# Attention and two MoE layers on one core: loads of q and k in three parts, and the copy of the tails behind VectorE's decoding step

## The chip, the cores and the metric

The kernel runs on one core of a Trainium2 chip. The metric is the device time of one execution in microseconds; an execution that was profiled has, beside its time, a span from its first to its last instruction. TensorE multiplies matrices, VectorE, ScalarE and GpSimd work on elements, and SyncE issues nearly all of the DMA transfers. Each of them runs its own instructions in order; between engines the order is kept by semaphores.

## The reference

All inputs are 32-bit floats; the weights of the two MoE layers are 64-bit floats that the kernel decodes itself. Cut to what is computed:

```python
scores = scale * np.matmul(q, k.transpose(0, 1, 3, 2))      # 4 batches, 8 heads, 576 rows, 64 wide
rel = (pos[:, None] - pos[None, :]).astype(np.float32)
x = (np.log1p(np.abs(rel)) / psi_i)[..., None]
bias = np.maximum(x @ w1 + b1, 0.0) @ w2                    # one bias for each head
scores = scores + bias.transpose(2, 0, 1)[None]
attn = np.exp(scores - scores.max(-1, keepdims=True))
attn = attn / (attn.sum(-1, keepdims=True) + 1e-09)
x = np.matmul(attn, v)                                      # then rows of 2304 tokens, 512 wide
h = np.maximum(np.maximum(x @ w1, x @ w2), x @ w3)          # first layer, 768 wide
x = h @ w_out
h = x @ w_in                                                # second layer, 2048 wide
out = np.where(h > 0, h, np.exp(np.minimum(h, 0)) - 1) @ w_out
```

## The kernel before

A prologue makes the bias and stores it in DRAM (to about 62 us of the profiled span). Then the attention runs (to about 335 us), then the first MoE layer (to about 626 us) and the second. The change touches the attention alone.

The attention has 16 pairs of heads, numbered n, and each has five steps, c = 0 to 4, so there are 80 steps s = 5n + c. Four of them have 128 query rows of both heads; c = 4 has the last 64 rows of both, in one half. The order of the work is written out by hand. Each piece of work is put on a list with a due time in steps (`at`, line 548); the list is sorted by that time (line 591), and each engine's queue is filled in that order. The due times set an order, not a clock: an engine starts its next instruction as soon as the semaphores allow it.

The pieces of step s that matter, with the table `OFF` (line 35), are these. `unit_qk` (line 216) has TensorE multiply q and k into the PSUM tile `PB[0]` for h = 0 and `PB[1]` for h = 1. `scores` (line 225) is VectorE's reduction of that product with the bias tile; it writes `e_t`. `expo` is ScalarE's exponential. `recip` and `diag` make reciprocals of sums (VectorE) and diagonal tiles (GpSimd, line 249). Two steps later `trans` transposes the exponentials into `TQ` on TensorE, and `tails` (line 262) transposes the last 64 columns into two spare 64-column corners of `PB[0]`. `evac_tails` (line 299) is VectorE's copy of these corners to SBUF; it is the 128x128 COPY of line 77 in the trace (64x128 in c = 1, which handles the tail of a c = 4 step). `evac` copies `TQ`: ScalarE does it, but VectorE does one half where the source step has c = 0 or 2, which falls into the running steps c = 2 and 4. `pv` multiplies by v, and `x_copy`, `x_sum`, `x_hi`, `x_lo` finish an output block, the last two on GpSimd (lines 73 and 81).

`pump` (line 471), due at 0.32 in every step from 7 on except c = 1, takes the decoder of the MoE weights one piece further. A piece is one VectorE instruction on 128x512 integers (lines 420, 423, 425, 427, 430, in turn), at times with a fetch of raw weights (line 371) or a store of finished ones (line 466) on SyncE's queue, and with ScalarE or GpSimd work of splitting.

So in one step VectorE's order is: scores of h = 0, reciprocals of the step before, in c = 0 and 2 the sum of an output block (line 345), scores of h = 1, copy of the tails (due at 2.311 of its own step, which is 0.311 in the running one), decoding piece (0.32), in c = 2 and 4 the copy of one half of `TQ`. TensorE's is: products of q and k for both h, transposes, tails, products with v, and then the products of the next step, whose first half writes `PB[0]` again.

`load_kq` (line 94) brings the 864 KB of q and k of a pair into one of two buffers, `load_v` (line 98) the 320 KB of v into one of two. They are due at 5n + 0.2 for the pair n + 1, and 5n + 6.2, which is one step into that pair. The tile of q and k has k in its first 576 columns and the two heads' q in the second and third 576.

Of the kernel before, what the change touches and what calls it, by code (L numbers as in the profile page):

```python
# [11 lines left out]
F32 = mybir.dt.float32  # L12
# [19 lines left out]

OFF = {"qk0": 0.0, "qk1": 0.01, "t0": 0.02, "ns": 1.025, "dg": 1.026, "t1": 0.03, "tr": 2.10, "tl": 2.20, "evt": 2.311,
       "pump": 0.32, "ev0": 2.385, "ev1": 2.387, "ex0": 0.38, "ex1": 0.40}
PV_AT = {1: [(4.5, 0), (4.5, 1), (5.5, 2), (5.5, 3), (5.5, 4)],
         4: [(3.5, 0), (3.5, 1), (4.5, 2), (4.5, 3), (5.5, 4)]}
# [15 lines left out]
def fused_kernel(ctx, tc, tkq, vv, lt, pk, wm1, wo1, win2, wo2, out):  # L54
    nc = tc.nc
# [34 lines left out]
    kq = att.enter_context(tc.tile_pool(name="kq", bufs=2))  # L90

    KQ, TV = {}, {}

    def load_kq(n):
        KQ[n] = kq.tile([128, 1728], F32, tag="kq", name="kq_t")
        nc.sync.dma_start(KQ[n], tkq[n])

    def load_v(n):
        TV[n] = ld.tile([128, 640], F32, tag="tv", name="tv_t")
# [21 lines left out]
    with ExitStack() as pro:  # L121
# [18 lines left out]
        with tc.manual_schedule():  # L140
            nc.sync.dma_start(pk_t, pk)
            nc.sync.dma_start(lt_t[:, 512:1148], lt[:, 512:1148])
            nc.sync.dma_start(lt_t[:, 0:512], lt[:, 0:512])
            load_kq(0)
            load_v(0)
            nc.vector.tensor_scalar(nbt, psi_t, b1_t, -1.0, op0=ALU.mult, op1=ALU.mult)
# [401 lines left out]
    def at(key, fn, *args):  # L548
        plan.append((key, len(plan), fn, args))

    for s, (n, c) in enumerate(steps):
        o = {nm: s + off for nm, off in OFF.items()}
        at(o["qk0"], unit_qk, s, 0)
# [22 lines left out]
        if n % 4 == 3 and n < 15:  # L576
            at(s + 0.45, load_b, n // 4 + 1, c)
    for n in range(4 * NP - 1):
        at(5 * n + 0.2, load_kq, n + 1)
        at(5 * n + 6.2, load_v, n + 1)  # L580
    at(3.05, fetch)
    at(3.05, fetch)
    for i in range(6):
# [317 lines left out]
```

## Time and profile before

| | us |
|---|---|
| median of 3 runs | 1014.34 |
| lowest and highest run | 1010.53, 1014.87 |
| profiled execution, its time | 1010.22 |
| its span | 1008.4 |
| TensorE busy in the span | 977.4 |
| VectorE busy | 692.1 |
| ScalarE busy | 526.1 |
| GpSimd busy | 341.7 |

Busy times are sums over the whole span, over stages with different limits. Below, TensorE is PE (its weight loads PEld), VectorE DVE, ScalarE ACT, GpSimd POOL, and SyncE's queue SPq. In a row of the timeline the numbers ahead are start and duration in microseconds, "xN" is how many instructions were merged into it, and a bracket at its end holds the engine's idle time before it and what ended that. "issue" in the chain of waits is time in which an engine waited for nothing that the profile shows.

### The profile page before, as it was taken

The page shows a single profiled execution, that of the slowest core. Times are in us where ns is not written, and L with a number is a line of the kernel's source. Part 1 is how long each engine was busy: PE and PEld are TensorE (multiplying, and loading weights), DVE is VectorE, ACT ScalarE, POOL GpSimd, SP SyncE. Part 2 cuts the span into 40 slices and gives each one's busy share as a digit, 9 for nine tenths or more (in the row PEclk, how much of TensorE's full clock was granted, in tenths as well). Part 3 has the DMA queues.
Part 4 walks back from the last instruction along what each step waited for, and adds up shares of the span by engine and source line. Part 5 has one row for each costly group of instructions (what it writes and reads, how often), then busy time and mean ns, then how long its engine had stood idle before and what let it go on. Part 6 is the DMA issues. An engine that isn't in the chain of part 4 may idle for free.

```text
span 1008.4 us, 28525 instructions
## 1 busy us (share of the span) xinstructions
PE 977.4 (97%) x11748; PEld 869.2 (86%) x11748; DVE 692.1 (69%) x1428; ACT 526.1 (52%) x1087; POOL 341.7 (34%) x419
## 2 busy tenths in 40 slices
PE   7979899999999999999999999999999999999998
PEld 4447777778887899999999999998998989988996
DVE  7967778788886699887887862835574355743342
ACT  8967777777775233333333331644445344453443
POOL 0013344344343354534553550323232132321222
PEclk9989999999999999999999999999999999999999
DMA  7842724645532356879886981355657556575553
GB/s 259 291 172 85 247 94 157 205 163 187 176 127 79 134 187 215 308 234 341 321 282 236 328 298 47 116 189 175 199 192 252 191 171 204 188 258 185 176 197 105
DMA packets 65905, 201.00 MB, mean 199 GB/s; under 512 B 7024, under 2 KB 14832, under 8 KB 65776
## 3 DMA queue, kind: packets, MB, share of 16 engines
q1 hardware_dynamic: 65776, 199.18, 57.6%
q8 instruction: 93, 1.52, 0.6%
q14 instruction: 36, 0.29, 0.1%
HBM read 150.78 MB, written 48.37 MB: 197 GB/s over the span
## 4 chain that ended last, share of the span: by engine, by line
PE 91%; DVE 6%; issue 1%; DMA 1%; ACT 0%; SPq 0%; POOL 0%; DVEq 0%; POOLq 0%; ACTq 0%
PE xo L696 18%; PE pb L740 13%; PE pb L526 12%; PE tq L740 6%; PE tq L252 6%; PE xo L319 6%; PE xo L526 5%; PE tq L526 5%; PE pb L222 5%; PE pb L620 4%; PE pb L183 3%; PE pbb L183 2%; DVE e_t L230 2%; PE xo L620 2%; PE tq L620 2%
## 5 line engine op out<-in xcount | busy, mean ns | idle before, releaser
L81 POOL TENSOR_TENSOR gl<-t_t,gh 128x384 fp32r<-128x384 f32 x96 | 108.7, 1142 | 286.3 <-ACT gh L75 286.3
L235 ACT ACTIVATE e_t<-e_t,st_t 128x576 f32<-128x576 f32 x144 | 111.4, 773 | 58.6 <-DVE st_t L240 56.1
L230 DVE CUSTOM_DVE_ANT_0 e_t<-pb,b_t 128x576 f32<-128x576 f32 x144 | 107.7, 749 | 32.7 <-PE pb L222 32.5
L249 POOL TENSOR_SCALAR dg_t<-ident,st_t 128x64 f32<-128x64 f32 x144 | 48.1, 348 | 212.7 <-DVE st_t L241 93.2
L740 PE MATMUL pb<-w_t,gh 128*128 128x512 f32 x384 | 119.3, 392 | 0.0
L526 PE MATMUL pb<-xh,w_t 128*128 128x384 f32 x448 | 116.8, 336 | 0.0
L252 PEld LDWEIGHTS tq<-dg_t,e_t 64*64 64x64 f32 x4608 | 96.6, 136 | 22.7 <-issue 7.7
L252 PE MATMUL tq<-dg_t,e_t 64*64 64x64 f32 x4608 | 97.8, 222 | 10.9 <-issue 5.3
L696 PE MATMUL xo<-tt,w_t 128*128 128x384 f32 x528 | 107.4, 338 | 0.0
L718 ACT ACTIVATE t_t<-c_t 128x384 f32<-128x384 f32 x96 | 50.0, 521 | 103.4 <-DVE c_t L709 95.6
L222 PE MATMUL pb<-kq_t 64*64 64x288 f32 x1152 | 98.6, 413 | 3.8 <-issue 1.3
L696 PEld LDWEIGHTS xo<-tt,w_t 128*128 128x128 f32 x528 | 95.0, 188 | 7.7 <-issue 0.3
L696 PE MATMUL xo<-xh,w_t 128*128 128x384 f32 x328 | 94.6, 335 | 0.0
L319 PE MATMUL xo<-p,tv_t 64*64 64x320 f32 (+1 forms) x1024 | 85.4, 408 | 1.6 <-issue 1.2
L526 PEld LDWEIGHTS pb<-xh,w_t 128*128 128x128 f32 x448 | 81.1, 188 | 0.5 <-issue 0.4
L740 PEld LDWEIGHTS pb<-w_t,gh 128*128 128x128 f32 x384 | 70.5, 188 | 6.6
L740 PE MATMUL pb<-w_t,gl 128*128 128x512 f32 x192 | 75.5, 393 | 0.0
L526 PE MATMUL pb<-xl,w_t 128*128 128x384 f32 x224 | 75.3, 336 | 0.0
L75 ACT ACTIVATE p<-tq 128x512 f32<-128x512 f32 (+1 forms) x128 | 62.8, 528 | 16.4 <-PE tq L252 15.2
L222 PEld LDWEIGHTS pb<-kq_t 64*64 64x64 f32 x1152 | 50.9, 133 | 22.9 <-DVE p L77 4.4
L75 ACT ACTIVATE gh<-t_t 128x384 fp32r<-128x384 f32 x96 | 48.6, 519 | 33.4 <-DVE t_t L726 33.4
L696 PEld LDWEIGHTS xo<-xh,w_t 128*128 128x128 f32 x328 | 60.2, 188 | 3.0
(131 smaller groups left out, 2198.1 us busy)
## 6 DMA issues: line engine op xcount, KB each, us to landing
w_t<-scw_w SPq DMA_DIRECT2D x90, 512.0 KB, 4.4
w_t<-scw_wi SPq DMA_DIRECT2D x74, 512.0 KB, 4.2
kq_t<-tkq SPq DMA_DIRECT2D x16, 864.0 KB, 5.4
scw_wi<-sp SPq DMA_DIRECT2D x26, 512.0 KB, 4.7
scw_w<-sp SPq DMA_DIRECT2D x22, 512.0 KB, 5.5
raw<-wo SPq DMA_DIRECT2D x22, 512.0 KB, 3.7
scr<-o_t SPq DMA_DIRECT2D x36, 288.0 KB, 3.9
raw<-wm SPq DMA_DIRECT2D x18, 512.0 KB, 4.1
```

Source lines behind the costliest of these rows:

```text
L75: nc.scalar.activation(dst, src, AF.Copy)
L81: e.tensor_tensor(out=dst, in0=src, in1=hi.bitcast(F32), op=ALU.subtract)
L183: mm(p[32 * a4:32 * a4 + 32, 224 + 288 * hf:512 + 288 * hf], w28, FT[A, a4][:, 288 * hf:288 * hf + 288], start=True, stop=True)
L222: mm(PB[h][H64[g], 224 + 288 * r:512 + 288 * r], t[H64[r], 576 + 576 * a + q0:640 + 576 * a + q0], t[H64[r], 288 * a:288 * a + 288], start ...
L230: nc.vector.tensor_tensor_reduce(out=E[s][:, 576 * h:576 * h + 576], in0=PB[h][:, 224:800], in1=BT[n // 4, c, h], op0=ALU.add, op1=ALU.min ...
L235: nc.scalar.activation(e, e, AF.Exp, bias=st[:, h:h + 1], scale=-1.0, accum_out=st[:, 2 + h:3 + h])
L252: mm(dst, E[s][H64[g], k0:k0 + 64], DG[s][H64[g], h % nheads(s)], start=True, stop=True)
L319: mm(XO[g][H64[h], 0:w], v[H64[g], 128 * k + 64 * h:128 * k + 64 * h + 64], ps[0][H64[g], 4 * h + k, :], start=(k == 0), stop=(k == 3 and ...
L526: mm(ps[blk][:, 0:NB], wt[:, ks], xt[:, kk, t0:t0 + NB], start=(j == 0), stop=(j == 11))
L620: mm(ps[blk][:, 0:NB], WO[0][:, kk, wt, ms], xt[:, bs], start=(j == 0), stop=(j == 3 * NM1 - 1))
L696: mm(ps, w[wt][:, ks], b[xt][:, kk], start=(start and j == 0), stop=(stop and j == 5), skip_group_check=True)
L740: mm(acc[t], g[:, ts], w[k], start=(f == 0 and i == 0 and j == 0), stop=(f == NU - 1 and i == 1 and j == 2))
```

## The change

Two things are changed. The copy of the tails gets the due time 2.33 in place of 2.311, which is 0.33 in the running step and so behind the decoding piece at 0.32. The load of q and k is issued in three parts of 576 columns (288 KB each), due at 5n + 1.2, 2.2 and 3.2 in place of one of 864 KB at 5n + 0.2, and the load of v is due a step later, at 5n + 7.2.

```diff
-OFF = {... "tr": 2.10, "tl": 2.20, "evt": 2.311,
+OFF = {... "tr": 2.10, "tl": 2.20, "evt": 2.33,
        "pump": 0.32, "ev0": 2.385, "ev1": 2.387, "ex0": 0.38, "ex1": 0.40}
...
-    def load_kq(n):
-        KQ[n] = kq.tile([128, 1728], F32, tag="kq", name="kq_t")
-        nc.sync.dma_start(KQ[n], tkq[n])
+    def load_kq(n, i=None):
+        if not i:
+            KQ[n] = kq.tile([128, 1728], F32, tag="kq", name="kq_t")
+        cs = slice(576 * i, 576 * i + 576) if i is not None else slice(0, 1728)
+        nc.sync.dma_start(KQ[n][:, cs], tkq[n][:, cs])
...
     for n in range(4 * NP - 1):
-        at(5 * n + 0.2, load_kq, n + 1)
-        at(5 * n + 6.2, load_v, n + 1)
+        for i in range(3):
+            at(5 * n + 1.2 + i, load_kq, n + 1, i)
+        at(5 * n + 7.2, load_v, n + 1)
```

## Rows read from the trace of the kernel before

**Rows 1.** The page's first part: busy time, share of the span, instructions of each engine.

```profile
PE 977.4 (97%) x11748; PEld 869.2 (86%) x11748; DVE 692.1 (69%) x1428; ACT 526.1 (52%) x1087; POOL 341.7 (34%) x419
```

**Rows 2.** Busy time by stretch; columns: PE, PEld, DVE, ACT, POOL, clock, DMA, GB/s.

```profile
128.00:144.00 16.00, 15.94 (x485) 12.99 (x477) 14.07 (x43) 11.92 (x29) 6.12 (x14) 1.00 0.39 144
```

**Rows 3.** Waits of PEld, 60 to 340 us: total, times, longest.

```profile
PEld pb L222 <- DVE p L77: 4.4, 14, 0.6
```

**Rows 4.** Timeline of steps 21 and 22 (c = 1 and 2), DVE and PE.

```profile
130.05 0.28 DVE L77 COPY p<-pb 64x128 f32<-64x128 f32 x1
...
131.38 0.76 DVE L230 CUSTOM_DVE_ANT_0 e_t<-pb,b_t 128x576 f32<-128x576 f32 x1 [1.05 <-PE pb L222]
...
133.34 0.28 DVE L77 COPY p<-pb 128x128 f32<-128x128 f32 x1
...
133.54 0.68 DVE L425 SCALAR_TENSOR_TENSOR t_w<-raw,t_w 128x512 int32<-128x512 int32 x1
...
133.69 1.38 PE L222 MATMUL pb<-kq_t 64*64 64x288 f32 x16
134.14 0.68 DVE L77 COPY p<-tq 128x512 f32<-128x512 f32 x1
...
134.74 0.75 DVE L230 CUSTOM_DVE_ANT_0 e_t<-pb,b_t 128x576 f32<-128x576 f32 x1
```

**Rows 5.** Timeline of steps 23 and 24 (c = 3 and 4), DVE and PE.

```profile
136.41 0.29 DVE L77 COPY p<-pb 128x128 f32<-128x128 f32 x1
...
136.95 0.76 PE L222 MATMUL pb<-kq_t 64*64 64x288 f32 x8
...
137.77 0.76 DVE L230 CUSTOM_DVE_ANT_0 e_t<-pb,b_t 128x576 f32<-128x576 f32 x1 [0.47 <-PE pb L222]
...
139.00 0.29 DVE L77 COPY p<-pb 128x128 f32<-128x128 f32 x1 [0.19 <-PE pb L252]
...
140.41 0.75 DVE L230 CUSTOM_DVE_ANT_0 e_t<-pb,b_t 128x576 f32<-128x576 f32 x1
```

**Rows 6.** Timeline of step 30 (c = 0), DVE and POOL.

```profile
160.15 0.29 DVE L77 COPY p<-pb 128x128 f32<-128x128 f32 x1
160.19 0.87 POOL L81 TENSOR_TENSOR xl<-xf,xh 128x320 fp32r<-128x320 f32 x1
160.35 1.25 DVE L430 TENSOR_TENSOR t_w<-t_w,x_t 128x512 int32<-128x512 int32 x1
...
161.53 0.74 DVE L230 CUSTOM_DVE_ANT_0 e_t<-pb,b_t 128x576 f32<-128x576 f32 x1
```

**Rows 7.** Timeline of step 27 (c = 2), with GpSimd's split of a weight.

```profile
150.04 0.40 POOL L73 TENSOR_SCALAR xh<-xf 128x256 fp32r<-128x256 f32 x1
...
150.21 0.29 DVE L77 COPY p<-pb 128x128 f32<-128x128 f32 x1
150.41 1.28 POOL L81 TENSOR_TENSOR w_t<-t_w,w_t 128x512 fp32r<-128x512 f32 x1
150.41 1.56 DVE L423 TENSOR_SCALAR t_w<-raw 128x512 int32<-128x512 int32 x1
...
152.49 0.74 DVE L230 CUSTOM_DVE_ANT_0 e_t<-pb,b_t 128x576 f32<-128x576 f32 x1
```

**Rows 8.** Groups of DVE, 66 to 320 us: count, busy us, mean ns, idle.

```profile
L420 DVE TENSOR_SCALAR x_t<-raw 128x512 int32<-128x512 int32 x13 | 6.5, 505 | 0.0
```

**Rows 9.** Timeline of SyncE's queue: loads of one pair.

```profile
204.49 0.33 SPq L96 DMA_DIRECT2D kq_t<-tkq  x1
206.24 0.33 SPq L100 DMA_DIRECT2D tv_t<-vv  x1
```

**Rows 10.** Chain of waits, attention: start, us, what; three of twelve such pieces.

```profile
76.33 0.67 issue
...
210.64 1.15 issue
...
298.83 0.35 issue
```

More of the change, by code (lines that the diff above doesn't have):

```diff
@@ L30 @@
 BIG = 3.0e38
-OFF = {"qk0": 0.0, "qk1": 0.01, "t0": 0.02, "ns": 1.025, "dg": 1.026, "t1": 0.03, "tr": 2.10, "tl": 2.20, "evt": 2.311,
+OFF = {"qk0": 0.0, "qk1": 0.01, "t0": 0.02, "ns": 1.025, "dg": 1.026, "t1": 0.03, "tr": 2.10, "tl": 2.20, "evt": 2.33,
        "pump": 0.32, "ev0": 2.385, "ev1": 2.387, "ex0": 0.38, "ex1": 0.40}
```

## The prediction

> **What bounds the kernel now.** I read the page first, then busy time by stretch, then the chain of waits and the timeline of single attention steps. On the page PE is busy 97% of the span [rows 1], and inside the attention a quiet stretch shows 15.94 of 16 us [rows 2]. So whatever makes PE wait in the attention lengthens the whole, and the MoE stages behind are only shifted. The chain has PE nearly everywhere, with two kinds of exceptions: DVE pieces, and pieces named "issue", where PE stands still with no semaphore to wait for. Of the latter above 0.3 us there are twelve, from 76 to 299 us, and they sum to 9.6 us [rows 10].
>
> The timeline shows what ties two steps together. PE's products of q and k for the next step write the PSUM tile from which DVE copies the tails, and they wait for that copy: the waits name it [rows 3], and in step 22 the copy runs from 133.34 to 133.62 and the first product starts at 133.69 [rows 4]. I compared all 77 pairs of steps from 2 to 78: never does the product start sooner than 0.05 us after the copy's end, and in 55 it starts within 0.12 us of it. From the copy's start to the product it is 0.35 us, and from the product to the next scores on DVE 0.82 us (136.95 to 137.77) [rows 5]. Hence a loop: copy, products, scores, copy, with **1.17 us** from the copy's start to the next scores. The decoding piece now lies beside that stretch, behind the copy; DVE would otherwise wait there, as it does 1.05 us in the step without a piece [rows 4].
>
> **The swap on DVE.** It removes and adds no instruction. It puts the piece ahead of the copy, so the copy, and PE behind it, wait for the piece. Wherever the tails are there when the scores end, that is a serial cost; 40 of 58 steps with a piece have the copy without any idle time ahead. What I compare is the time from now's start of the copy to the next scores, now against (piece + 1.17).
>
> A two-input piece (lines 425, 427, 430) shows 0.68 us, but its successor starts after 0.60 (133.54 to 134.14) [rows 4]; I use 0.60.
> - c = 2: now 133.34 to 134.74, 1.40 us [rows 4]. Then 0.60 + 1.17 = 1.77: +0.37, eight times, +3.0.
> - c = 3: now 136.41 to 137.77, 1.36 us [rows 5]. Then 1.77: +0.41, eight times, +3.3.
> - c = 4: the copy now waits 0.19 us for the tails, so the piece can start at 138.81; the next scores come at 138.81 + 1.77 = 140.58 in place of 140.41 [rows 5]: +0.17, six times, +1.0.
> - c = 0: now 160.15 to 161.53, 1.38 us, with a piece that is stretched to 1.25 us beside GpSimd's instruction of 160.19 to 161.06 [rows 6]. If the piece, starting at 160.15, comes ahead of GpSimd, it takes 0.60: +0.39, eight times, +3.1. If it comes second, it ends where it ends now, the copy starts some 1.38 us late, and the step grows by 1.17: +9.4 in all. That is the largest unknown. The nearest row is 0.04 us on the side that wins; a start at the same time as GpSimd's lost [rows 7]. I take the win and keep the loss as a rival.
>
> Of this stretching the trace shows both signs: in step 27 the piece and GpSimd's split both start at 150.41 and the piece takes 1.56 us [rows 7]. The Trainium skill ("SBUF — State Buffer", section "SBUF: two separate sides") says that VectorE and GpSimd share a pair of ports as an exclusive lock, that whichever starts first keeps it for its whole instruction, and that the other fully blocks. The rows agree in that the later one waits. By that rule the 0.04 us decides for VectorE in c = 0; were it the other way, the second sum above would hold.
>
> The short pieces (line 420, mean 0.505 us with the stretched ones in it [rows 8], some 0.35 us to the successor in an undisturbed one) cost +0.39 in three steps of c = 0, +0.2 in three of c = 2, +0.1 to +0.2 in five of c = 3 and 4: +2.5. The pieces of line 423 cancel. In c = 2 (three times) the piece would now start at 150.21, wait for GpSimd's instruction that ends at 150.44 and be done at about 150.67, ahead of the split; now the next scores come 2.28 us after the copy's start [rows 7], then 0.46 + 1.17 = 1.63: -0.65 each, -1.9. In two steps of c = 0 GpSimd's split is already running and the piece would hold the copy to its end: +2.4. The rest, with the few steps in which the copy waits for late tails (there the piece is free), I count at -0.5. Sum over the steps with a piece: 3.0 + 3.3 + 1.0 + 3.1 + 2.5 + 0.0 = **+12.9 us**, or +21.6 if c = 0 goes the other way, with 0.8 us more for each of the three short pieces there.
>
> In c = 1, with no piece, DVE now waits for a PE that is still busy, 130.05 to 131.38, 1.33 us [rows 4]. A PE that has waited a step earlier has no arrears; 1.33 - 1.17 = 0.16, fifteen times: **-2.4 us**.
>
> **The loads.** They sit on SyncE's queue, which nothing holds to the due times: today's load of q and k starts as soon as its buffer is free, and v follows 1.75 us later, when v's buffer is free (204.49, 206.24) [rows 9]. After the change the first part waits for the same event, the second stands behind v in the queue and the third behind it, so mostly it becomes 288 KB at once and the other 576 KB together with v 1.75 us later. Really a step apart they are only where a fetch, a store or a bias load, which themselves wait for DVE or GpSimd, stand between them: in pairs 3, 7 and 11 and about every second other pair. The two more issues a pair cost SyncE 0.33 us each, and it idles. The last part is due 1.8 steps, some 5.5 us, before its use, and it is put behind the decoder's fetch or store of c = 2, which waits for a piece of the step before. I cost this at nothing, since no product of q and k waits for a load today; if that cover were gone, PE would stand at the first product of a pair for as long as the last part is late, visible as a wait for that DMA.
>
> What the loads may give is in the issue gaps. Six of the twelve, 5.5 of 9.6 us, begin 4 to 7 us after a load of q and k was issued, as the gap at 210.64 after the load of 204.49 [rows 9, 10]. Instructions come by DMA as well; smaller bursts should shorten that delay. A slower PE also needs its instructions later. The bounds are 0 and -9.6 us; since the burst mostly only moves, I take **-4 us**. The Trainium skill ("Runtime: NRT & Kernel Launch", section "Instruction fetch mechanics") says that the fetch of instructions is hidden because the sequencer issues more slowly than they arrive; the gaps here speak against it, and by that rule the loads would bring nothing, 4 us more than my sum.
>
> **Sum.** +12.9 - 2.4 - 4 = +6.5 us. On the profiled execution (span 1008.4 us, time 1010.2 us) that is 1016.7 us. The median of the runs is 4.1 us above that execution, so I predict **1021 us** for the median.
>
> **Rivals.**
> - *The port is lost in c = 0.* Another +8.7: about 1030 us. For it: the margin of 0.04 us and the loss at equal starts [rows 6, 7]. Chance 0.20.
> - *The gaps go altogether.* If all 9.6 us vanish, +12.9 - 2.4 - 9.6 = +0.9: about 1015 us. For it: six gaps follow a load of q and k. Against: the same bytes come within the same few us. Chance 0.16.
> - *The piece becomes free and the kernel faster.* If PE's tails came later than 0.60 us after the end of the scores, the piece would fill a wait of DVE, and the next scores would follow the copy by 1.17 us in place of 1.40, 1.36 and 1.38: about -0.2 in up to 44 steps, -9 us, with the loads -13: 1001 us if it held everywhere, about 1006 if in half of the steps. For it: a few steps after gaps have such late tails now. Against: the copy follows the scores without idle time in most steps. Chance 0.12.
> - That the loads don't come a step apart is in my sum already.
>
> **How the numbers follow.** My forecast has a chance of 0.52, with a range of its own from 1015 to 1026 us. About 0.5% is what a measurement of this kernel can tell from no change: below 1009.3 is faster, above 1019.4 slower. Faster is the third rival, 0.12. Within 0.5% are the second rival and a quarter of the forecast, 0.29. Slower is the rest, 0.59. The range from 1009 to 1031 us leaves out most of the third rival and the upper part of the first.
>
> **What would show it.** In the trace of the changed kernel the piece should start right after the second scores, the copy after it, and the first product 0.07 us after the copy; waits of PE and PEld at line 222 for the copy should grow from about 5 us to 15 or more. The issue gaps should sum to 3 to 8 us. In c = 0 the piece should show 0.68 us, not 1.25. Wrong I would be if the product didn't wait for the copy, or if PE's time in the attention fell.

## The result, and the profile after

| | before | changed |
|---|---|---|
| median, us | 1012.39 | 1025.53 |
| lowest and highest of 6 runs | 1009.45, 1014.87 | 1022.96, 1026.45 |
| profiled execution, its time | 1010.22 | 1025.00 |
| its span | 1008.4 | 1023.2 |

The changed kernel is slower: the ratio is 1.0127, with a 95% interval from 1.0103 to 1.0151, or 13.1 us between the medians. Three more runs of before have brought its median down from 1014.34 us. The prediction was 1021.0 us, inside a range from 1009 to 1031; it had the direction and the mechanism of the swap, but only half of the loss (+6.7 us on its median). The forecast time is nearer to the result (4.5 us) than the forecast loss (6.4 us), because it was set on that higher median; on 1012.39 us the same +6.7 us would give 1019.1 us.

The first part of the page of the changed kernel, and the shares in its chain of waits:

```profile
PE 982.1 (96%) x11748; PEld 856.0 (84%) x11748; DVE 685.6 (67%) x1428; ACT 525.7 (51%) x1087; POOL 342.1 (33%) x419
...
PE 86%; DVE 10%; issue 2%; DMA 1%; ACT 1%; POOL 0%; SPq 0%; DVEq 0%; POOLq 0%; ACTq 0%
```

As many instructions stand on each engine as in [rows 1], and DVE is even busy 6.5 us less, yet DVE has 10% of the chain, where the page of before gives it 6%. So DVE has no more work; its work stands in a place where PE waits for it. The waits say where (columns: who <- what, total us, times, longest; 60 to 350 us; two lines were added to the program, so line 224 here is 222 of before):

```profile
PEld pb L224 <- DVE p L77: 37.0, 52, 3.4
PE pb L224 <- DVE p L77: 14.5, 30, 2.8
```

In [rows 3] the first of these was 4.4 us in 14 waits. The second, before (60 to 340 us):

```profile
PE pb L222 <- DVE p L77: 1.2, 3, 0.4
```

I cut both traces into the lengths of the steps, from one step's first scores to the next step's. From step 2 to step 78 they sum to 14.71 us more. Behind the attention nothing changed: from the end of the last scores to the end of the span it is 691.9 us before and 692.2 us after. The whole loss lies in the attention.

The timeline of steps 22 to 24 of the changed kernel (start, duration, instruction, in a bracket the idle time before it) shows the same pieces of work as [rows 4, 5]:

```profile
135.85 0.77 DVE L427 SCALAR_TENSOR_TENSOR t_w<-raw,t_w 128x512 int32<-128x512 int32 x1
136.54 0.28 DVE L77 COPY p<-pb 128x128 f32<-128x128 f32 x1
136.74 0.68 DVE L77 COPY p<-tq 128x512 f32<-128x512 f32 x1
...
136.87 1.20 PE L224 MATMUL pb<-kq_t 64*64 64x288 f32 x16 [0.26 <-DVE p L77]
...
137.65 0.76 DVE L232 CUSTOM_DVE_ANT_0 e_t<-pb,b_t 128x576 f32<-128x576 f32 x1 [0.24 <-PE pb L224]
...
139.34 0.69 DVE L429 SCALAR_TENSOR_TENSOR t_w<-raw,t_w 128x512 int32<-128x512 int32 x1
139.94 0.28 DVE L77 COPY p<-pb 128x128 f32<-128x128 f32 x1
...
141.06 0.76 DVE L232 CUSTOM_DVE_ANT_0 e_t<-pb,b_t 128x576 f32<-128x576 f32 x1 [0.84 <-PE pb L224]
...
142.03 0.67 DVE L432 TENSOR_TENSOR t_w<-t_w,x_t 128x512 int32<-128x512 int32 x1
142.61 0.28 DVE L77 COPY p<-pb 128x128 f32<-128x128 f32 x1
...
143.74 0.76 DVE L232 CUSTOM_DVE_ANT_0 e_t<-pb,b_t 128x576 f32<-128x576 f32 x1 [0.24 <-PE pb L224]
```

The piece is first, the copy follows 0.58 to 0.69 us later, and the first product starts 0.05 us after the copy's end (136.82 to 136.87). From the piece to the next scores it is 1.80 us in c = 2 and 1.72 us in c = 3, where the forecast had 1.77 for both, and where before the copy led to the next scores in 1.40 and 1.36 us. What was beside the products now stands ahead of them; DVE idles 0.84 us behind the copy in c = 3, time that the piece used to fill.

### The profile page after: what moved, and what is told of

It reads as the page before. It is cut to its first block, busy times and chain, and to the rows that moved or that the text cites. A ratio compares the mean times of both kernels' runs of the same rounds, so it can differ in the third digit from the quotient of the medians.

```text
span 1023.2 us, 28563 instructions
## 1 busy us (share of the span) xinstructions
PE 982.1 (96%) x11748; PEld 856.0 (84%) x11748; DVE 685.6 (67%) x1428; ACT 525.7 (51%) x1087; POOL 342.1 (33%) x419
## 4 chain that ended last, share of the span: by engine, by line
PE 86%; DVE 10%; issue 2%; DMA 1%; ACT 1%; POOL 0%; SPq 0%; DVEq 0%; POOLq 0%; ACTq 0%
PE xo L699 17%; PE pb L743 13%; PE pb L528 11%; PE pb L224 6%; PE tq L743 6%; PE xo L528 5%; PE tq L528 5%; DVE e_t L232 4%; PE tq L254 4%; PE xo L321 4%; PE pb L623 4%; PE pb L185 3%; PE pbb L185 2%; PE xo L623 2%; PE tq L623 2%
## 5 line engine op out<-in xcount | busy, mean ns | idle before, releaser
L224 PE MATMUL pb<-kq_t 64*64 64x288 f32 x1152 | 94.1, 417 | 16.4 <-DVE p L77 14.5
L254 PEld LDWEIGHTS tq<-dg_t,e_t 64*64 64x64 f32 x4608 | 89.9, 136 | 22.5 <-issue 6.7
L254 PE MATMUL tq<-dg_t,e_t 64*64 64x64 f32 x4608 | 90.1, 220 | 9.0 <-issue 4.7
L224 PEld LDWEIGHTS pb<-kq_t 64*64 64x64 f32 x1152 | 43.2, 133 | 51.0 <-DVE p L77 37.0
```

The source lines that it names most:

```text
L224: mm(PB[h][H64[g], 224 + 288 * r:512 + 288 * r], t[H64[r], 576 + 576 * a + q0:640 + 576 * a + q0], t[H64[r], 288 * a:288 * a + 288], start ...
L254: mm(dst, E[s][H64[g], k0:k0 + 64], DG[s][H64[g], h % nheads(s)], start=True, stop=True)
```

## The experiments

Each is compared with runs of before on the same chip; numbers in brackets are 95% intervals of the ratio.

**The swap alone, and the loads alone.** The first question is which of the two parts costs the time.

```diff
-OFF = {... "evt": 2.311,
+OFF = {... "evt": 2.33,
```

> The swap alone, loads as before. Theory (the decoding piece is in series with the copy of the tails, and the products of the next step wait for the copy): nearly all of the loss, 11 to 15 us above the kernel before, steps with a two-input piece longer by 0.35 to 0.40 us in c = 0, 2 and 3. Rival (the loads, which now fall into the stretches with bias loads, make half of the loss): 5 to 8 us above.

Measured: 1026.21 us against 1010.84, ratio 1.0148 [1.0132, 1.0165], +15.4 us. The swap by itself carries the whole loss.

The second kernel has the loads of the change, in three parts and a step later, with the copy at 2.311 as before.

```diff
-    def load_kq(n):
-        KQ[n] = kq.tile([128, 1728], F32, tag="kq", name="kq_t")
-        nc.sync.dma_start(KQ[n], tkq[n])
+    def load_kq(n, i=None):
...
-        at(5 * n + 0.2, load_kq, n + 1)
-        at(5 * n + 6.2, load_v, n + 1)
+        for i in range(3):
+            at(5 * n + 1.2 + i, load_kq, n + 1, i)
+        at(5 * n + 7.2, load_v, n + 1)
```

> The loads in three parts alone, order on VectorE as before. Theory: within 2 us of the kernel before, issue gaps on TensorE between 7 and 10 us in all. The prediction had -4 us here, by fewer gaps. Rival (the loads make half of the loss): 5 to 8 us above.

Measured: 1014.14 us against 1010.84, ratio 1.0032 [1.0018, 1.0046]. The loads alone cost 3.3 us and gain nothing. The gaps named "issue" (here: PE's waits of over 0.15 us, between 64 and 345 us) sum to 9.6 us in the profiled execution, beside 9.5 us of before: the -4 us of the prediction isn't there. They have become 8 instead of 12, but longer, up to 2.8 us:

```profile
PE tq L254 <- issue: 6.1, 4, 2.8
...
PE pb L254 <- issue: 3.4, 4, 1.6
```

**One instruction more, ahead of the copy or behind it.** My theory was that only the place ahead of the copy costs. The rival was that DVE has become the bound, so that any work more on it costs. Both kernels give DVE one more two-input instruction of the size of a piece in each of fifteen steps of c = 1, which have no piece; they differ only in its place.

```diff
+    dum = const.tile([128, 512], I32, name="dum")
...
+    def extra():
+        nc.vector.tensor_tensor(out=dum, in0=dum, in1=dum, op=ALU.bitwise_or)
...
+    for s, (n, c) in enumerate(steps):
+        if s > 5 and c == 1:
+            at(s + 0.305, extra)      # second kernel: s + 0.315
```

> The kernel before with one more two-input VectorE instruction on 128x512 integers in each step of c = 1 from step 6 on (15 of them, 0.6 us each; it changes no result), put ahead of the copy of the tails. Theory: the step grows from 3.02 to about 3.4 us, as (piece + 1.17) takes the place of 1.33, so +5 to +7 us. Rival (any work added to VectorE costs its own time, since VectorE is near its bound): the same as the kernel with the instruction behind the copy.

> The same 15 instructions, put behind the copy of the tails. Theory: they lie beside TensorE's first products of the next step, in VectorE's idle 1.05 us, and cost nothing: within 2 us of the kernel before. Rival: the same cost as ahead of the copy, 5 to 9 us in both.

Measured: ahead 1015.15 us, ratio 1.0044 [1.0029, 1.0059]; behind 1012.29 us, ratio 1.0013 [0.9998, 1.0027], both against 1010.84. The steps tell it more sharply: ahead, an undisturbed step of c = 1 (one with no gap named "issue" near it, in either kernel) grows from 3.02 to 3.40 us (+0.37 to +0.40); behind, by 0.00 within 0.02. Step 21 on DVE, ahead and then behind:

```profile
129.94 0.69 DVE L581 TENSOR_TENSOR dum<-dum 128x512 int32<-128x512 int32 x1
130.54 0.28 DVE L79 COPY p<-pb 64x128 f32<-64x128 f32 x1
131.65 0.76 DVE L232 CUSTOM_DVE_ANT_0 e_t<-pb,b_t 128x576 f32<-128x576 f32 x1 [0.84 <-PE pb L224]
```

```profile
129.11 0.28 DVE L79 COPY p<-pb 64x128 f32<-64x128 f32 x1
129.31 0.67 DVE L581 TENSOR_TENSOR dum<-dum 128x512 int32<-128x512 int32 x1
130.44 0.76 DVE L232 CUSTOM_DVE_ANT_0 e_t<-pb,b_t 128x576 f32<-128x576 f32 x1 [0.46 <-PE pb L224]
```

Ahead, the next scores come 1.71 us after the instruction's start; behind, 1.33 us after the copy's start, exactly as without it [rows 4], and DVE still has 0.46 us to spare. The same instruction (0.69 and 0.67 us) costs 0.38 us in the one place and nothing in the other. DVE as the bound falls. Fifteen times 0.38 is 5.7 us, while the whole kernel shows 4.3 us more; the interval of the ratio reaches from 2.9 to 6.0 us.

**The copy taken out of the loop.** If the loop through `PB[0]` is what costs, then tails written to `PB[1]`, with the copy later in the step, should free PE.

```diff
+    def pbi(s):
+        return s == NS - 1 or s < NS - 3
...
-            return [PB[s == NS - 1][:, 64:128], PB[s == NS - 1][:, 832:896]]
+            return [PB[pbi(s)][:, 64:128], PB[pbi(s)][:, 832:896]]
...
-        at(o["tl"], tails, s)
+        at(o["tl"] if s >= NS - 3 else s + 2.6, tails, s)
-        at(o["evt"], evac_tails, s)
+        at(o["evt"] if s >= NS - 3 else s + 2.63, evac_tails, s)
```

> Loads as in the kernel before. The piece stays ahead of the copy on VectorE, but the tails go into the corners of PB[1] in place of PB[0], and TensorE makes them behind its products with v (due 2.6, the copy 2.63; the last three steps as before). So the copy no longer holds the products of h = 0 of the next step, only those of h = 1. Theory (the loss is the piece in series with these products): the loss of the swap is gone, between 10 us faster and 3 us slower than the kernel before. Rival (VectorE near its bound pays for the order as such): 10 to 15 us above, as the swap alone.

Measured: 1027.39 us against 1011.54, ratio 1.0159 [1.0136, 1.0182]. The expectation was missed. Its waits (60 to 340 us) show why it is no test:

```profile
DVE p L77 <- PE pb L252: 24.8, 26, 3.0
DVE p L77 <- PE xo L326: 15.1, 13, 2.8
PE pb L222 <- DVE p L77: 10.8, 24, 2.8
PE tq L252 <- issue: 7.1, 7, 1.6
PE xo L322 <- issue: 5.8, 3, 2.4
```

The products of the other half now wait for the copy, 10.8 us in 24 waits, and DVE stands before its copies for TensorE's products (the first two rows). Its gaps named "issue" grew to 17.6 us as well. Three things were moved at once (the tile, the tails, the copy), so it decides nothing on the loop; it shows only that this way out has a wait of its own.

**What the loads of q and k cost at all.** This kernel leaves them out from the third pair on, and computes with the q and k of the first two pairs.

```diff
-        t = KQ[n]
+        t = KQ[n % 2]
...
-        at(5 * n + 0.2, load_kq, n + 1)
+        if n == 0:
+            at(5 * n + 0.2, load_kq, n + 1)
```

> The kernel before without the loads of q and k from the third pair on; all pairs use the q and k of the first two, so the output is not the reference's. Theory of the prediction (bursts of q and k delay TensorE's instructions): the issue gaps in the attention, 9.5 us now, fall to 4 or 5 us, and the time by 4 to 6 us. Rival (the gaps come from the other transfers, the bias and weights above all): gaps of 8 to 10 us and the time within 2 us.

Measured: 1007.89 us against 1011.54, ratio 0.9968 [0.9951, 0.9984], -3.7 us. The gaps fall from 9.5 us to 6.4 us in 6 places, not to the 4 or 5 us expected:

```profile
PE tq L252 <- issue: 4.3, 4, 1.9
...
PE xo L319 <- issue: 1.2, 1, 1.2
...
PE pb L252 <- issue: 0.9, 1, 0.9
```

So the loads of q and k have a part in the time, and all of it together is worth some 0.3%. The fall of the gaps by 3.1 us is from one execution each, and two executions of one kernel differ by up to 2.4 us in this sum (below). The -4 us that I had put on a mere rearrangement of them was about all that taking them away gives.

**Split without moving, moved without splitting.** The two halves of the change to the loads, each alone: first three parts, all at the old due time (with `load_kq` in parts as above).

```diff
-        at(5 * n + 0.2, load_kq, n + 1)
+        for i in range(3):
+            at(5 * n + 0.2, load_kq, n + 1, i)
```

> The load of q and k in three parts, all three at the old due time, v as before; order on VectorE as before. Loads in parts and moved were 0.32% slower than the kernel before. If splitting is the cost: again 2 to 4 us slower. If moving is: within 1.5 us of the kernel before.

Then one load of 864 KB, a step later, with v a step later too.

```diff
-        at(5 * n + 0.2, load_kq, n + 1)
-        at(5 * n + 6.2, load_v, n + 1)
+        at(5 * n + 1.2, load_kq, n + 1)
+        at(5 * n + 7.2, load_v, n + 1)
```

> The loads of q and k whole, but due a step later, v a step later too; order on VectorE as before. If moving them behind and among the bias loads of pairs 3, 7 and 11 is the cost: 2 to 4 us slower than the kernel before, with longer issue gaps in these pairs. If splitting is: within 1.5 us.

Measured: split 1011.66 us, ratio 1.0005 [0.9990, 1.0020]; moved 1018.46 us, ratio 1.0078 [1.0057, 1.0099], both against 1011.54. Splitting alone does nothing. Moving alone costs 6.9 us, and the gaps of its profiled execution are 16.7 us, 7.2 us more than before:

```profile
PE tq L252 <- issue: 11.2, 10, 2.5
...
PE pb L252 <- issue: 4.5, 3, 3.1
```

The waits of PE for the copy of the tails are 2.5 us there and 14.5 us in the changed kernel, so this loss has no part in the other mechanism. With the parts alone (+0.78%, +0.05%) and both together (+0.32%), the split gives back more than half of what the move costs. What ends the gaps can be read from the traces' records of DMA packets, in which instructions are a kind of their own (16 KB each on queue q8). All 12 gaps of before and all 15 here end 1.2 to 1.6 us after such a packet has landed, where about one moment in ten lies so by chance. So in these gaps TensorE waits for its instructions. Why a later load makes them longer isn't settled: two of the longest (2.5 and 3.1 us, at 120 and 126 us) follow the bias loads of pair 3, but one of 2.3 us at 297 us has no bias load near it, and which transfer delays the instructions was not tried.

**Short pieces.** If the length of the piece is the loss, a quarter of it should be nearly free. With the swap, the pieces of weights 3 to 12 work on 128 columns only; the other three quarters of these weights aren't decoded, ScalarE fills them.

```diff
-OFF = {... "evt": 2.311,
+OFF = {... "evt": 2.33,
...
+            cw_ = lambda z: z[:, 0:128] if 2 <= i < 12 and lim[0] == 12 else z
-            nc.vector.tensor_tensor(out=t, in0=t, in1=x, op=ALU.bitwise_or)
+            nc.vector.tensor_tensor(out=cw_(t), in0=cw_(t), in1=cw_(x), op=ALU.bitwise_or)
```

> The swap alone, with VectorE's decoding pieces of the weights 3 to 12, which fall into the attention, cut from 512 to 128 columns; ScalarE fills the rest with other numbers, so those weights and the output are not the reference's. Theory (the cost of the swap is the piece's own length in series): with a piece of about 0.2 us in place of 0.6 the next scores come 0.2 + 1.17 us after the scores' end, as in the kernel before, so the loss goes: between 6 us faster and 3 us slower than the kernel before. Rival (the order as such, or the copy's place, costs): 8 us or more above.

Measured: 1022.46 us against 1011.79, ratio 1.0100 [1.0083, 1.0116], +10.7 us. For the total the expectation was missed. In the single steps it held: with a short two-input piece an undisturbed step takes what it took before, or less: c = 0 -0.03 to -0.06 us, c = 2 +0.01, c = 3 +0.07 to +0.09, c = 4 -0.27 to -0.28. Step 22 on DVE:

```profile
134.95 0.37 DVE L429 SCALAR_TENSOR_TENSOR t_w<-raw,t_w 128x128 int32<-128x128 int32 x1
135.24 0.28 DVE L77 COPY p<-pb 128x128 f32<-128x128 f32 x1
135.44 0.68 DVE L77 COPY p<-tq 128x512 f32<-128x512 f32 x1
136.36 0.76 DVE L230 CUSTOM_DVE_ANT_0 e_t<-pb,b_t 128x576 f32<-128x576 f32 x1 [0.24 <-PE pb L222]
```

From the piece to the next scores it is 1.41 us, with 1.40 us before [rows 4] and 1.80 us in the changed kernel. The copy follows the piece after 0.29 us in place of 0.69, and the 0.40 us between the two are what the step had lost. So the loss of a step goes with the length of the piece. What is left of the total has other places: the last four steps, whose pieces had their full length (+3.85 us); the pieces of the first weights, also of full length (about +1); two steps of c = 0 where the piece waits for GpSimd's split (+0.93, +0.91); the start (+1.2); and gaps of 13.1 us in place of 9.5, with one step that grew by 4.1 us. Why the gaps grew stays open, and so this run settles the price of a step but not the sum.

**The change and the swap side by side.** Do the loads add or give back anything beside the swap? The changed kernel and the swap alone, as above, were run together on one chip.

> The changed kernel again, on the same chip as the swap alone. If the loads in parts add their 3 us beside the swap too: 1 to 5 us above the swap alone. If TensorE's waits for the copy take them up: within 2 us of it, some 13 to 15 us above the kernel before.

> The swap alone again, to be compared with the changed kernel on the same chip: 13 to 16 us above the kernel before.

Measured: changed 1022.85 us, ratio 1.0112 [1.0094, 1.0130]; swap alone 1024.87 us, ratio 1.0135 [1.0118, 1.0152], both against 1011.79. The changed kernel is 2.0 us lower, and the intervals overlap. The loads cost nothing beside the swap, though alone they cost 3.3 us; whether they give back 2 us isn't settled. Their gaps are 6.0 and 6.6 us, while other executions of the same two kernels have 8.4 and 8.8: one profiled execution places such a sum to some 2 us only. The 7.2 us of the moved load are well beyond that.

**The last four steps.** Steps 75 to 78 of the changed kernel grew by 0.99, 0.52, 1.02 and 0.61 us, more than one two-input piece explains. The trace has two pieces in step 75 and three in step 77, before as after; the program has loads for the first MoE layer due at 74.39 (line 42), and that these pull the pieces together is my reading, not tested. Step 77 of the changed kernel, on DVE:

```profile
322.48 0.51 DVE L425 TENSOR_SCALAR t_w<-raw 128x512 int32<-128x512 int32 x1
324.14 0.93 DVE L425 TENSOR_SCALAR t_w<-raw 128x512 int32<-128x512 int32 x1 [1.15 <-POOL sp L81]
325.11 0.69 DVE L427 SCALAR_TENSOR_TENSOR t_w<-raw,t_w 128x512 int32<-128x512 int32 x1
325.71 0.28 DVE L77 COPY p<-pb 128x128 f32<-128x128 f32 x1
325.91 0.68 DVE L77 COPY p<-tq 128x512 f32<-128x512 f32 x1
326.84 0.76 DVE L232 CUSTOM_DVE_ANT_0 e_t<-pb,b_t 128x576 f32<-128x576 f32 x1 [0.24 <-PE pb L224]
```

Three pieces, and a wait of 1.15 us for GpSimd's split, all stand ahead of the copy. To see what this is worth, the last run has the swap in all steps but these.

```diff
-        at(o["evt"], evac_tails, s)
+        at(s + 2.33 if s < 73 else o["evt"], evac_tails, s)
```

> The swap alone, but not in the last steps of the attention: copies of source steps from 73 on keep their old place. In steps 75 to 78 the kernel with the swap alone is longer than the kernel before by about 4 us in the profile, as loads for the first MoE layer pull several decoding pieces into one step, and all of them then stand ahead of the copy. Theory: 3 to 4 us of the loss go, so 9 to 12 us above the kernel before, with steps 75 to 78 as long as before. Rival (these steps only shift waits that come later anyway): 13 to 15 us above, as with the swap everywhere.

Measured: 1022.38 us against 1010.92, ratio 1.0123 [1.0107, 1.0139], +11.5 us. Steps 75 to 78 are back to what they were, within 0.02 us; the swap alone in the comparison above has +0.99, +0.52, +1.41 and +1.53 there. The same step 77, with the copy ahead:

```profile
320.07 0.28 DVE L77 COPY p<-pb 128x128 f32<-128x128 f32 x1
320.28 1.56 DVE L423 TENSOR_SCALAR t_w<-raw 128x512 int32<-128x512 int32 x1
321.76 0.68 DVE L77 COPY p<-tq 128x512 f32<-128x512 f32 x1
322.36 0.41 DVE L423 TENSOR_SCALAR t_w<-raw 128x512 int32<-128x512 int32 x1
322.80 0.69 DVE L425 SCALAR_TENSOR_TENSOR t_w<-raw,t_w 128x512 int32<-128x512 int32 x1
323.41 0.75 DVE L230 CUSTOM_DVE_ANT_0 e_t<-pb,b_t 128x576 f32<-128x576 f32 x1
```

From the end of the scores to the next ones it is 3.34 us here and 4.36 us in the changed kernel. By the steps, the end of the attention is worth 3.1 us of the loss in the changed kernel and 4.4 us in the swap alone; by the totals it is +11.5 us against +13.1 and +15.4 for the swap alone, whose intervals touch this one's.

Of the kernels that load all of q and k none beats the one before; the most that these loads could give is the 0.3% of the run without them.

## Why the prediction was right, and where its sizes were off

**The loop and the price of a piece: right.** That the piece and the copy now stand in series with the products is shown by the timeline, by the waits (PE from 1.2 us to 14.5, PEld from 4.4 to 37.0), by the instruction added ahead and behind, and by the short pieces. The steps with two-input pieces, forecast and measured (undisturbed steps):

| source of the piece's step | forecast, us | measured, us |
|---|---|---|
| c = 0 | +0.39 | +0.34 to +0.37 |
| c = 2 | +0.37 | +0.40 |
| c = 3 | +0.41 | +0.37 to +0.38 |
| c = 4 | +0.17 | +0.03 to +0.05 (+0.14 in step 9) |

With the forecast's counts of steps these sizes give 9.2 us, where 10.4 was forecast. The loop was 0.05 us too long in the forecast: in 50 of the 58 steps with a piece the next scores follow the copy after 1.11 to 1.13 us, not 1.17. That c = 2 came out all the same is luck: there the copy follows the piece after 0.69 us, not 0.60, in steps in which GpSimd's instruction of line 73 still runs when the piece starts. Mis-sized was c = 4: I had its piece start 1.04 us after the scores of 137.77 [rows 5]. In the timeline of the changed kernel above it starts 0.97 us after them (141.06 to 142.03), the copy follows 0.58 us later in place of 0.60, and the next scores 1.13 us after that in place of 1.17: 0.13 us less than worked out.

**The short pieces and line 423: near in sum.** In undisturbed steps a short piece cost +0.35 us in c = 0, +0.23 to +0.26 in c = 2, +0.11 to +0.13 in c = 3 and +0.03 in c = 4, some 1.9 us up to step 74; the forecast had 2.5, with step 75 in it. Line 423 gave -0.74 and -0.73 us in c = 2 (forecast -0.65 each), and +1.12 and +1.11 us in two steps of c = 0 in which the piece waits for GpSimd's split (forecast +1.2 each); with its other steps some +0.9 us up to step 74, where the forecast had 0.0 with step 77 in it. The third step of c = 2 was step 77, above, with +1.02.

**The port in c = 0: the choice held.** The rival with a price of 8.7 us didn't occur, nor did that of a piece that becomes free: no undisturbed step with a two-input piece got shorter. Step 30 of the changed kernel, DVE, POOL and PE:

```profile
161.80 0.69 DVE L432 TENSOR_TENSOR t_w<-t_w,x_t 128x512 int32<-128x512 int32 x1
...
161.84 1.37 POOL L81 TENSOR_TENSOR xl<-xf,xh 128x320 fp32r<-128x320 f32 x1
...
162.41 0.28 DVE L77 COPY p<-pb 128x128 f32<-128x128 f32 x1
...
162.75 1.20 PE L224 MATMUL pb<-kq_t 64*64 64x288 f32 x16 [0.40 <-DVE p L77]
```

The piece starts 0.04 us ahead of GpSimd's instruction and takes 0.69 us, not the 1.25 us of [rows 6]; now GpSimd's takes 1.37 us in place of 0.87. By the lock that the Trainium skill ("SBUF — State Buffer", section "SBUF: two separate sides") describes, the later of the two waits for the whole instruction of the earlier. The two traces show both orders, and in each the later one is stretched, though by somewhat less than the whole rest of the earlier: by 0.50 us here, with 0.65 us of the piece left, and by 0.57 us in [rows 6], with 0.71 us of GpSimd's instruction left.

**The recovery in c = 1: wrong.** The step that failed is "A PE that has waited a step earlier has no arrears", with -2.4 us. The eight steps of c = 1 up to 71 that no gap disturbs in either trace have the same length as before, within 0.02 us; step 16 is 0.34 us longer, with a gap of 0.11 us that is too short to be counted above. The 1.33 us from the copy to the next scores were no arrears of the step before: PE has this step's own products with v to do beside the first products of q and k. Step 21 of the changed kernel, PE and DVE:

```profile
132.56 0.28 DVE L77 COPY p<-pb 64x128 f32<-64x128 f32 x1
...
132.90 0.46 PE L224 MATMUL pb<-kq_t 64*64 64x288 f32 x2
132.94 0.38 PE L325 MATMUL xo<-p,tv_t 64*64 64x256 f32 x1
...
133.89 0.76 DVE L232 CUSTOM_DVE_ANT_0 e_t<-pb,b_t 128x576 f32<-128x576 f32 x1 [1.06 <-PE pb L224]
```

Here too the first product starts 0.06 us after the copy's end (132.84 to 132.90), but the next scores come 0.99 us after it, where it is 0.78 us in step 22 (136.87 to 137.65). The copy still leads to the next scores in 1.33 us, and the waiting of 1.05 us in [rows 4] is 1.06 us here. PE's work in a step, not its arrears, fills that stretch.

**The end of the attention: left out.** I took one piece for each step. In steps 75 to 78 there are several, with a wait for GpSimd between them, and they cost 3.1 us in the changed kernel. The trace of before shows these pieces too.

**The loads: wrong.** The step that failed is "smaller bursts should shorten that delay", with -4 us. Alone they cost 3.3 us; beside the swap the difference to the swap alone is -2.0 us, within the intervals. The gaps of the changed kernel are 8.4 us, just outside the 3 to 8 that the prediction named, and 6.0 us in another execution. That six gaps follow a load of q and k was right as an observation, but without these loads there are still 6.4 us of gaps. What the Trainium skill ("Runtime: NRT & Kernel Launch", section "Instruction fetch mechanics") says, that the fetch of instructions is hidden, would let neither the gaps nor a change of 7.2 us in them come from loads alone; the kernel with the moved load speaks against it, and so do the packets of instructions that end the gaps. So what the prediction said of the gaps, that they are waits for instructions, holds; that smaller bursts shorten them does not: in three parts at the old time the kernel kept its time (1.0005) and its gaps (9.3 us). For the loads alone, "the loads bring nothing", which I had given as the outcome by that rule, came closer than my own term; beside the swap both are 2 us off.

**The account.** The sum of +6.5 us was worked out on the profiled execution, and there 14.8 us were measured (1025.00 against 1010.22); between medians it is 13.1. The pieces up to step 74 came to some 12 us (9.2, 1.9 and 0.9), with 12.9 forecast for all of them; the last four steps brought another 3.1. The recovery of 2.4 us doesn't exist. The gaps gave 1.1 us in place of 4. That is 14 us; the rest is below what two executions of one kernel differ by. So the large term was nearly right, and the total was short because both terms that were to take something off it failed and the end was left out. That the median still lies inside the range says little: from 1009 to 1031 us the range also held no change at all.

## What to carry to other kernels

Where an engine does its list in order, as DVE does here, put first the instruction for which the bounding engine waits, and the filler behind it: the same instruction on DVE cost 0.38 us in a step ahead of the copy and nothing behind it. When such an order changes, go through every step in which the moved item occurs, the last ones too, and count how many of them are drawn into one step. Before a term is given to moved transfers, ask what taking them away altogether would bring: here that was 0.3%.

## What was not expected of the hardware

A small margin between two starts decides which of DVE and GpSimd is stretched. In the eight steps of c = 0 with a two-input piece, the piece took 1.25 to 1.27 us where it started 0.16 us behind GpSimd's instruction, and 0.69 us where it started 0.04 us ahead; then GpSimd's took 1.37 us in place of 0.87. DVE's copies from PSUM beside GpSimd's work keep their 0.28 to 0.29 us. The same 864 KB, issued a step later, lengthened PE's stands at "issue" from 9.5 to 16.7 us, and in three parts brought them back to 9.6 us, while three parts at the old time changed nothing. And these stands are waits for instructions: each ends 1.2 to 1.6 us after a 16 KB packet of instructions has landed.
